# A deeper software pipeline and another weight conversion in a fused top-k attention and MLP kernel

## The chip, the cores and the metric

The kernel runs on one core of a Trainium2 chip. The metric is device time of one execution in microseconds (us). The kernel before took 1919.19 us (median of 3 runs, 1914.49 to 1919.27).

Engines are named as in the profile: PE is TensorE (matmuls and transposes; PEld its weight loads), DVE is VectorE, ACT is ScalarE, POOL is GpSimd, SP is SyncE, which here issues every DMA. Each engine works through its own instructions in a fixed order and waits in place when an operand or a buffer isn't ready, so what stands behind a waiting instruction waits too.

## The reference

Eight batches of eight heads, 576 positions, head size 64. Each row of scores keeps its 32 largest; the rest get weight zero. The attention output goes through an MLP with 512 inputs, 2048 hidden units and 512 outputs.

```python
scores = scale * np.matmul(q, k.transpose(0, 1, 3, 2))
kth = np.partition(scores, -top_k, axis=-1)[..., -top_k:-top_k + 1]
scores = np.where(scores >= kth, scores, -1000000000.0)
attn = np.exp(scores - np.max(scores, axis=-1, keepdims=True))
attn = attn / (np.sum(attn, axis=-1, keepdims=True) + 1e-09)
x = np.matmul(attn, v)            # then (B,H,S,D) -> (B*S, H*D)
h = x @ w_in
g = np.where(h >= 1, h, np.where(h <= -1, 0.0, (h + 1) ** 2 / 4))
return g @ w_out
```

The two weight matrices arrive as 64-bit floats. The kernel loads each number as two 32-bit words and builds a 32-bit float from them itself.

## The kernel before

**Steps.** A step is 128 query rows of a pair of heads (`hp`), or 64 tail rows of two pairs. There are 144 steps, 18 for each batch. `begin` (with `scores`, L221) makes the scores of a step on PE in two halves of 288 keys; ACT scales them out of PSUM into `s` (L224; a ring of three). `weights` is DVE's part: the maximum of each column pair (`more`, L238), four rounds of the eight largest values and their removal (L244, L251), the minimum of each pair (`less`, L256) and its eight largest (L259), the 32nd value (`kth`, L263), then the mask, which multiplies the exponentials by "score is at least kth" and sums them (L271), and the reciprocal of the sum (L276, L277). ACT computes the exponentials `e` (L248) as soon as the first maximum stands, and POOL divides `e` by its sum (L279). `transpose_w` turns `e` on PE (L290, L293; ACT copies to `wT` and `wTt`, L291, L294), and `values` multiplies with v (L305, L313; ACT copies to `xT`, L318, L320).

**MLP.** When all steps of a chunk (one or two tiles of 128 rows) are done, its MLP joins a list `pending` in units: 16 hidden groups `hidden(f)` (four matmuls over 128 or 256 columns, L336; ACT reads the result twice, L340 and L342; POOL finishes the activation, L343 to L345), then the output in pairs of f (`final`, L353, 512 columns).

**Order.** PE's and DVE's instructions are put out in program order; ACT, POOL and SP are ordered by a scheduler. The main loop runs over m, and in one turn puts out: the values of step m-2, the scores of step m+1, DVE's `weights` of step m, half of the MLP share, the weight transposes of step m-1, query and key transposes for later steps, the other half of the share. The share is the MLP work left over the turns left; `advance` puts out units while their cost is covered, and only those whose weight pieces are already converted.

**Weight conversion.** 64 pieces of 256 columns are converted while the first steps run; `weights` calls `between()` six times in a step and each call converts one piece. A piece has three operations on DVE (L85, L86, L90), two passes on POOL (L93, L94), two on ACT (L92, L97), and a last one on DVE (L99), which is put out after the next piece's first three. Four pieces are put out ahead of step 0.

**PSUM.** Eight banks: four for the tag "a", shared in rotation by scores, weight, key and query transposes and `po` (the values' result), three for `ph` (hidden), one for `py` (output).

**End.** After everything the largest entry of `excess` is found (L478 to L483), and a flag decides whether a slower variant runs; in these runs it doesn't.

## Time and profile before

| | |
|---|---|
| median of 3 runs | 1919.19 us (1914.49 to 1919.27) |
| the profiled execution | 1915.05 us, of which its span 1913.0 us |
| granted TensorE clock, mean | 0.942 |
| PE busy in the span | 1679.1 us (88%) |
| DVE busy | 1625.4 us (85%) |
| POOL busy | 1028.8 us (54%) |
| ACT busy | 977.1 us (51%) |
| DMA | 57.75 MB, mean 30 GB/s |
| chain that ended last | PE 53%, DVE 22%, POOL 13%, ACT 6% of the span |

The span runs from the first to the last instruction. Busy time is time in which an engine executed something; two engines can be busy at once. The granted clock is the share of full speed that the clock gate gave TensorE: at a lower one the same matmuls take longer and look busier. Matmuls are pipelined, so one busy engine can still hold several of them. A row such as `PE pw L290 <- POOL e L279` says that PE's instruction of line 290, writing `pw`, was released last by POOL's of line 279, writing `e`; the numbers behind it are total us, times and the longest. In a timeline a row has start, duration, engine, line, operation, what it writes and reads, and shapes.

### The profile page before, as it was taken

The numbers are of one execution on the slowest core, as the hardware profiler recorded it, in microseconds if no ns is written. First come the engines' busy times: TensorE is split into PE (matmuls) and PEld (weight loads), VectorE is DVE, ScalarE is ACT, GpSimd is POOL, SyncE is SP. The second block draws the span as 40 slices with busy tenths as digits, with TensorE's granted clock in tenths as the row PEclk, the third lists the DMA queues.
The fourth block names the chain that finished last, engine by engine and source line by source line (L and its number), as shares of the span: only waits on it lengthen the run. The fifth ranks groups of instructions, "written<-read, shape, count | busy, mean of one in ns | idle before, by whom it ended". The sixth has DMA issues, their size and how long they took to land.

```text
span 1913.0 us, 32251 instructions
## 1 busy us (share of the span) xinstructions
PE 1679.1 (88%) x10129; PEld 1160.1 (61%) x10129; DVE 1625.4 (85%) x5011; ACT 977.1 (51%) x2429; POOL 1028.8 (54%) x1772
## 2 busy tenths in 40 slices
PE   2346478898999999998999999998999999998998
PEld 1234255656676685767575776666676667666565
DVE  5998989999999799999898898989987879879640
ACT  4345455546455564655454655555455555445432
POOL 3567572725454672818283674637274554553553
PEclk8667679899999999999999999999999999998999
DMA  6222210011010000110010000110010000000000
GB/s 173 80 78 77 77 28 17 26 30 24 9 40 20 23 18 23 32 36 12 16 38 23 21 12 24 40 27 12 23 31 25 11 12 11 10 12 7 6 7 14
DMA packets 107445, 57.75 MB, mean 30 GB/s; under 512 B 86272, under 2 KB 94464, under 8 KB 107264
## 3 DMA queue, kind: packets, MB, share of 16 engines
q1 hardware_dynamic: 107264, 55.59, 10.6%
q8 instruction: 82, 1.34, 0.3%
q14 instruction: 99, 0.81, 0.1%
HBM read 46.14 MB, written 9.44 MB: 29 GB/s over the span
## 4 chain that ended last, share of the span: by engine, by line
PE 53%; DVE 22%; POOL 13%; ACT 6%; issue 5%; DMA 1%; POOLq 0%; SPq 0%; DVEq 0%; ACTq 0%
PE py L353 24%; PE ph L336 11%; PE sp L221 6%; DVE tops L244 6%; PE po L305 5%; DVE more L251 5%; PE pw L290 4%; POOL g L345 4%; POOL r L344 3%; POOL e L279 2%; POOL r L343 2%; DVE e L271 2%; DVE more L238 2%; DVE seconds L259 2%; DVE less L256 1%
## 5 line engine op out<-in xcount | busy, mean ns | idle before, releaser
L353 PE MATMUL py<-w_out,g 128*128 128x512 f32 x1152 | 534.7, 607 | 41.7 <-DVE w_out L99 37.1
L336 PE MATMUL ph<-xT,w_in 128*128 128x256 f32 (+1 forms) x2816 | 553.3, 353 | 3.9 <-ACT g L342 2.8
L336 PEld LDWEIGHTS ph<-xT,w_in 128*128 128x128 f32 x2816 | 466.4, 197 | 83.0 <-issue 29.4
L244 DVE MAX8 tops<-more 128x8 f32<-128x288 f32 x1152 | 468.5, 448 | 5.0
L353 PEld LDWEIGHTS py<-w_out,g 128*128 128x128 f32 x1152 | 209.2, 191 | 286.4 <-issue 219.8
L251 DVE MATCH_REPLACE8 more<-tops,more 128x288 f32<-128x288 f32 x864 | 375.9, 443 | 0.0
L279 POOL TENSOR_SCALAR e<-e,rz 128x576 f32<-128x576 f32 x288 | 242.4, 850 | 130.9 <-DVE rz L277 104.9
L340 ACT ACTIVATE r<-ph,half 128x256 f32<-128x256 f32 (+1 forms) x352 | 153.9, 437 | 264.2 <-POOL g L345 135.2
L264 POOL TENSOR_TENSOR excess<-seconds,kth 128x2 f32<-128x2 f32 x144 | 39.2, 273 | 417.3 <-DVE kth L263 416.4
L271 DVE SCALAR_TENSOR_TENSOR e<-s,kth,e 128x576 f32<-128x576 f32 x288 | 242.4, 875 | 23.1 <-ACT e L248 6.6
L345 POOL TENSOR_TENSOR g<-r,g 128x256 f32<-128x256 f32 (+1 forms) x352 | 246.7, 701 | 24.0
L291 ACT COPY wT<-pw 128x512 f32<-128x512 f32 x288 | 155.5, 594 | 202.3 <-PE pw L290 202.3
L290 PE MATMUL pw<-ident,e 128*128 128x128 f32 x1152 | 161.5, 284 | 110.6 <-POOL e L279 105.9
L248 ACT ACTIVATE e<-s,nmax 128x576 f32<-128x576 f32 x288 | 213.1, 786 | 75.2 <-POOL nmax L246 74.4
L238 DVE TENSOR_TENSOR more<-s 128x576 f32<-128x576 f32 x144 | 130.4, 905 | 139.0 <-ACT s L224 138.6
L344 POOL TENSOR_TENSOR r<-r 128x256 f32<-128x256 f32 (+1 forms) x352 | 230.4, 655 | 26.1
L290 PEld LDWEIGHTS pw<-ident,e 128*128 128x128 f32 x1152 | 138.0, 146 | 162.5 <-POOL e L279 118.2
L221 PE MATMUL sp<-kT,qT 64*128 64x288 f32 x1024 | 196.5, 442 | 34.7 <-ACT xT L318 26.4
L224 ACT ACTIVATE s<-sp 128x288 f32<-128x288 f32 x576 | 197.9, 417 | 40.7 <-PE sp L221 36.8
L343 POOL TENSOR_SCALAR r<-r 128x256 f32<-128x256 f32 (+1 forms) x352 | 155.4, 441 | 93.5 <-ACT r L340 93.2
L305 PEld LDWEIGHTS po<-wT,v_in 128*64 128x64 f32 x2048 | 118.0, 140 | 74.8 <-issue 40.0
L221 PEld LDWEIGHTS sp<-kT,qT 64*128 64x128 f32 x1024 | 109.1, 189 | 84.6 <-ACT xT L318 39.4
(61 smaller groups left out, 1592.7 us busy)
## 6 DMA issues: line engine op xcount, KB each, us to landing
q_in<-in_q_dram SPq DMA_DIRECT2D x32, 256.0 KB, 3.0
v_in<-in_v_dram SPq DMA_DIRECT2D x8, 1024.0 KB, 5.8
k_in<-in_k_dram SPq DMA_DIRECT2D x64, 128.0 KB, 3.0
raw<-in_moe_w_in_dram SPq DMA_DIRECT2D x32, 256.0 KB, 2.7
raw<-in_moe_w_out_dram SPq DMA_DIRECT2D x32, 256.0 KB, 2.8
out_dram<-y SPq DMA_DIRECT2D x32, 256.0 KB, 2.3
v_tail<-in_v_dram SPq DMA_DIRECT2D x16, 64.0 KB, 2.5
k_tl<-in_k_dram SPq DMA_DIRECT2D x8, 128.0 KB, 3.2
```

Source lines behind the costliest of these rows:

```text
L221: nc.tensor.matmul(o[:, a0 - c0:a1 - c0], qT[d, g, :], kT[d, g, k0:k0 + a1 - a0], start=True, stop=True)
L244: nc.vector.max(out=tops[:, i, r:r + 8], in_=src[:, i, :])
L248: nc.scalar.activation(e[:, i, :], s[:, i, :], AF.Exp, bias=nmax[:, i:i + 1])
L251: nc.vector.match_replace(out=rest[:, i, :], in_to_replace=tops[:, i, r:r + 8], in_values=src[:, i, :], imm_value=LOWEST)
L271: nc.vector.scalar_tensor_tensor(out=e[:, i, :], in0=s[:, i, :], scalar=last[:, i:i + 1], in1=e[:, i, :], op0=ALU.is_ge, op1=ALU.mult, acc ...
L279: nc.gpsimd.tensor_scalar(e[:, i, :], e[:, i, :], rz[:, i:i + 1], 1.0, ALU.mult, ALU.mult)
L290: nc.tensor.transpose(pt[:, c, :], w[:, i, main(i)][:, c * P:(c + 1) * P], ident)
L305: nc.tensor.matmul(po[j * D:(j + 1) * D], v_in[:, h, c, :] if c < NT else v_tl[0][:, h, :], wT[:, j, c, :] if c < NT else wTt, start=(c == ...
L336: nc.tensor.matmul(ph, w_in[:, kk, f * P:(f + 1) * P], xT[:, kk, 0:cw], start=(kk == 0), stop=(kk == NK - 1))
L344: nc.gpsimd.tensor_tensor(out=r, in0=r, in1=r, op=ALU.mult)
L345: nc.gpsimd.tensor_tensor(out=g[:, 0:cw], in0=r, in1=g[:, 0:cw], op=ALU.add)
L353: nc.tensor.matmul(py, gs[f][:, i * P:(i + 1) * P], w_out[:, f, :], start=(f == 0), stop=(f == NF - 1))
```

## The change

It has six parts.

1. **A further step between mask and transposes.** In turn m the weight transposes are those of step m-2 and the values those of step m-3 (before: m-1 and m-2). `e` gets three buffers. The MLP share of a turn is put out as a quarter, a quarter and a half, and query and key transposes now stand ahead of the weight transposes. `advance` has a second condition: it keeps running times of PE and DVE from constants, and puts out units also while PE's is short of the time at which the `e` to be transposed is done.
2. **The next step's pair maxima ahead of the mask.** `more` of step m+1 is put out before the mask of step m. `less` is written over `more`, which gets two buffers.
3. **An own bank for values.** `po` leaves the tag "a" for a bank of its own. `ph` becomes two tiles of one bank each, each holding two hidden groups, in place of three tiles of one group. `y` has one buffer instead of two.
4. **Another conversion.** A piece has one operation on DVE, one on ACT with a bias, one integer add on POOL and one more on ACT, then two on DVE. The last two of a piece are put out ahead of the next piece's first part. Seven pieces a step for four steps, then eight; two calls ahead of step 0 instead of four. `raw` has three buffers.
5. **Early first scores.** Keys of the first head pair are loaded first, the values of a batch after its last keys. The first step's scores are put out after the first of four key blocks, with ACT in program order for that part.
6. **The check of `excess`** is put out in the last turn but one, ahead of the last MLP units.

The core of the diff:

```diff
     def weight_piece(pool, dst, src):
-        raw = pool.tile([P, 2 * WC], U32, name="raw", bufs=2)
+        raw = pool.tile([P, 2 * WC], U32, name="raw", bufs=3)
...
-        nc.vector.tensor_scalar(top, hi, 3, 0x3FFFFFFF, ALU.logical_shift_left, ALU.bitwise_and)
-        nc.vector.scalar_tensor_tensor(out=top, in0=hi, scalar=0xC0000000, in1=top,
-                                       op0=ALU.bitwise_and, op1=ALU.bitwise_or)
-        nc.vector.tensor_scalar(unit, top, 0xFF800000, None, ALU.bitwise_and)
-        nc.scalar.activation(low, lo, AF.Copy, scale=2.0 ** -52)
-        nc.gpsimd.tensor_tensor(out=low, in0=low, in1=unit.bitcast(F32), op=ALU.mult)
-        nc.gpsimd.tensor_tensor(out=low, in0=low, in1=top.bitcast(F32), op=ALU.add)
+        nc.vector.tensor_scalar(bits, hi, 3, None, ALU.logical_shift_left)
+        nc.scalar.activation(units, lo, AF.Identity, bias=two, scale=2.0 ** -51)
+        nc.gpsimd.tensor_tensor(out=bits.bitcast(I32), in0=bits.bitcast(I32), in1=units.bitcast(I32), op=ALU.add)
         nc.scalar.activation(size, hi.bitcast(F32), AF.Abs)
         yield
-        nc.vector.scalar_tensor_tensor(out=dst, in0=size, scalar=1.125 * 2.0 ** -15, in1=low,
+        nc.vector.scalar_tensor_tensor(out=bits, in0=hi, scalar=0x80000000, in1=bits,
+                                       op0=ALU.bitwise_and, op1=ALU.bitwise_or)
+        nc.vector.scalar_tensor_tensor(out=dst, in0=size, scalar=1.125 * 2.0 ** -15, in1=bits.bitcast(F32),
                                        op0=ALU.is_ge, op1=ALU.mult)
...
             piece = weight_piece(pool, dst, src)
-            next(piece)
             if before is not None:
                 next(before, None)
-                yield
+            next(piece)
             before = piece
+            yield
...
         def keys_of(b):
-            v_in, v_tl = load_values(b)
...
+                if hp == NHP - 1:
+                    got["v"], got["v_tl"] = load_values(b)
...
+        def pairs(st):
+            s = st["s"]
+            st["more"] = more = att.tile([P, 2, SH], F32, name="more")
+            nc.vector.tensor_tensor(out=more, in0=s[:, :, 0:SH], in1=s[:, :, SH:S], op=ALU.max)
...
-            st["e"] = e = att.tile([P, 2, S], F32, name="e")
+            st["e"] = e = att.tile([P, 2, S], F32, name="e", bufs=3)
...
-                src = rest = more
+                src = rest = less = st["more"]
...
+            if paired and after is not None:
+                pairs(after)
             z = att.tile([P, 2], F32, name="z")
...
-            po = ps.tile([P, P], F32, name="po", tag="a", bufs=4)
+            po = ps.tile([P, P], F32, name="po", tag="po")
...
-                ph = ps.tile([P, CW], F32, name="ph", tag="ph", bufs=3)[:, 0:cw]
+                if f % 2 == 0:
+                    phs.append(ps.tile([P, 2, CW], F32, name="ph", tag="ph", bufs=2))
+                ph = phs[-1][:, f % 2, 0:cw]
...
-                    y = pool.tile([P, DM], F32, name="y", bufs=2)
+                    y = pool.tile([P, DM], F32, name="y", bufs=1)
...
+        K_TIME, PIECE_TIME, UNIT_TIME = 10.2, 1.3, 0.22
+        pe_time, dve_time, done = 8.0, 10.0, {}
+        def advance(amount, until=0.0):
             due += amount
-            while pending and pending[0][1] <= converted and due >= pending[0][0]:
+            while pending and pending[0][1] <= converted and (due >= pending[0][0] or
+                                                              pe_time + pending[0][0] * UNIT_TIME < until):
                 cost, _, work = pending.popleft()
-                due -= cost
+                due = max(due - cost, 0.0)
                 spent += cost
+                pe_time += cost * UNIT_TIME
                 work()
...
-        queries(0)
-        begin(0)
-        for _ in range(4):
-            convert()
+        with tc.manual_schedule(engines={mybir.EngineType.Activation}):
+            queries(0)
+            begin(0)
+            if paired:
+                convert()
+                convert()
+                pairs(state[0])
+            for _ in first:
+                pass
...
-        for m in range(n + 2):
-            if 2 <= m:
-                values(state[m - 2])
+        for m in range(n + 3):
+            if 3 <= m:
+                values(state[m - 3])
...
-                weights(state[m], convert)
-            advance(share / 2)
-            if 1 <= m <= n:
-                transpose_w(state[m - 1])
+                quota, before = (7 if m < 4 else 8), converted
+                def between():
+                    slots[0] += 1
+                    while converted - before < quota * slots[0] // 6 and converted < n_pieces:
+                        convert()
+                weights(state[m], state[m + 1] if m + 1 < n else None, between)
+                dve_time = max(dve_time, pe_time if m == 0 else 0.0) + K_TIME + PIECE_TIME * (converted - before)
+                done[m] = dve_time
+            advance(share / 4)
             queries(m + 2)
...
-            advance(share / 2)
+            advance(share / 4, done.get(m - 2, 0.0) + 2.5)
+            if 2 <= m <= n + 1:
+                pe_time = max(pe_time, done[m - 2] + 2.0) + 1.0
+                transpose_w(state[m - 2])
+            if m == n + 1 and paired:
+                judge(ps, att)
+            advance(share / 2, pe_time + 1.5)
```

## Prediction

> **What bounds the kernel now.** I read the page's 40 slices first, one digit for the busy tenths of a slice of 48 us.
>
> ```profile
> PE   2346478898999999998999999998999999998998
> DVE  5998989999999799999898898989987879879640
> PEclk8667679899999999999999999999999999998999
> ```
>
> In slices 2 to 6 VectorE (DVE) is at eight or nine tenths while TensorE (PE) is at two to six, on a granted clock of six to eight tenths; from slice 9 on PE is nearly always full. So there are two stages with two limits. The table of busy time by stage, cut at step boundaries, gives the sizes (columns: stage, length, then busy time and instructions of PE, weight loads, DVE, ACT, POOL, then granted clock).
>
> ```profile
> 0.00:30.56 30.56, 11.18 (x48) 8.09 (x48) 8.33 (x20) 14.50 (x34) 8.62 (x21) 1.00 0.77 202
> 30.56:140.76 110.20, 32.75 (x208) 24.70 (x208) 104.28 (x287) 45.63 (x119) 67.79 (x97) 0.62 0.32 88
> 140.76:252.00 111.24, 56.01 (x270) 34.85 (x270) 103.78 (x283) 48.18 (x125) 72.65 (x111) 0.70 0.24 71
> 252.00:327.00 75.00, 67.45 (x472) 48.86 (x472) 66.47 (x213) 42.26 (x110) 36.30 (x75) 0.93 0.06 17
> 327.00:1873.00 1546.00, 1480.65 (x8969) 1022.48 (x8970) 1341.63 (x4211) 815.63 (x2008) 825.58 (x1423) 0.98 0.08 21
> ```
>
> Before 30.56 no attention step has begun on DVE. From there to 252, ten steps plus the weight conversion fill DVE to 94%. After 327 PE is busy 1480.65 of 1546 us, so 65.3 us is all that better overlap can win there. The waits of PE after 324 us say what they are (total, times, longest).
>
> ```profile
> PE sp L221 <- ACT xT L318: 24.6, 21, 5.2
> PE pk L182 <- ACT wT L291: 11.8, 7, 3.8
> PE pw L290 <- POOL e L279: 9.1, 6, 3.1
> PE sp L221 <- ACT xT L320: 5.7, 6, 1.7
> PE py L353 <- ACT y L357: 4.6, 6, 0.9
> ```
>
> Last I read DVE's timeline for one converted weight piece, and for the pair maximum right after a piece and in a step without pieces.
>
> ```profile
> 100.85 0.28 DVE L85 TENSOR_SCALAR top<-raw 128x256 uint32<-128x256 uint32 x1
> 101.17 0.43 DVE L86 SCALAR_TENSOR_TENSOR top<-raw,top 128x256 uint32<-128x256 uint32 x1
> 101.63 0.29 DVE L90 TENSOR_SCALAR unit<-top 128x256 uint32<-128x256 uint32 x1
> 101.84 0.42 DVE L99 SCALAR_TENSOR_TENSOR w_in<-size,low 128x256 f32<-128x256 f32 x1
> 102.17 0.81 DVE L244 MAX8 tops<-more 128x8 f32<-128x288 f32 x2
> ...
> 116.54 1.29 DVE L238 TENSOR_TENSOR more<-s 128x576 f32<-128x576 f32 x1
> ```
> ```profile
> 302.06 0.76 DVE L238 TENSOR_TENSOR more<-s 128x576 f32<-128x576 f32 x1
> ```
>
> A piece takes 102.17 - 100.85 = 1.32 us, by starts 0.32 + 0.46 + 0.21 + 0.33. The same maximum takes 1.29 us beside POOL's second conversion pass (L94) and 0.76 without it.
>
> **The early stage, step by step.** Steps start on DVE (L238) at 30.56, 51.95, 73.34, 95.05, 116.54, 140.76, 166.02, 188.57, 210.06, 232.37, and step 16 at 322.75; a bare step takes 10.35 (302.06 to 312.41). A step with six pieces takes 21.5 = 10.35 + 6 x 1.32 + 3.2. The 3.2 are collisions with POOL, readable as 0.5 each on the pair maximum, the pair minimum and z, and about 1.4 on the last piece beside POOL's normalization of e.
>
> Start. The first key transpose (10.84) waits for a block issued only at 7.80, behind 1 MB of values. Now it is second in SP's queue: issue near 1.9, landing 2.95 later, transposes near 5. Copies as in the trace (two of 0.585, tail 0.74, queries 0.59), scores 3 us, so scores stand near 12 instead of 23. Then piece 0 goes through ACT (0.44), POOL (0.8) and DVE (0.46 + 0.33 + 0.32), so the first pair maximum starts near 14.5, 16 us earlier, but with one piece done instead of four. The values, moved behind the keys, are first used near 53; their 5.9 us are hidden, and lost if the first values wait for them. For later batches v_in (5.8 us) is issued some six steps later than now and still tens of us ahead of use.
>
> Pieces. DVE loses `unit`: 1.32 - 0.21 = 1.11 us. POOL loses one of two passes (788 and 836 ns). Its new integer add isn't in the trace: at least the one-input pass L343 on this shape (441 ns), at most both old passes (1624). I take 0.80, the nearest row being the old add. With 1624, POOL's load in an eight-piece step is 8 x 1.62 + 2.4 = 15.4 of 21 us, still hidden, but the collisions return, 1.4 x 9 = 13 us. ACT's conversion with a bias is priced as without (436; L340 has 437 with one; 422 to 594 by L97 and L291, off the path either way). The pair maximum now follows small operations, so its 0.5 goes. I take 2.3 of collisions instead of 3.2.
>
> Sum. Seven pieces: 10.35 + 7.8 + 2.3 = 20.4; eight: 21.5. 14.5 + 4 x 20.4 + 4 x 21.5 = 182; three pieces are left, 14.2, so 196. The first MLP tile cost steps 4 and 5 together 6.4 extra (24.2 and 25.3 against 21.5); I keep 6: 202. Seven bare steps more: step 16 starts at 275, not 322.75. PE's first two-tile hidden group starts at 329.77 now. After the change the scores ahead of it are those of step 19, whose buffer (three in the ring) is free only after the mask of step 16: 285.4 + 1.2, so 286.6, with two more steps' scores (2.4 us) already done. **Early gain: 43 + 2.4, say 46 us.** Cover: until then both single tiles must be done. Call a row what PE does up to one step's weight transposes. At full clock its scores, transposes and values take 3.8 us (1.2 + 1.2 + 1.4), a single tile 29 (16 hidden groups of 0.95, 16 output groups of 0.87: twelve L353 instructions in 5.3). Rows 8 to 15 of the changed PE order hold 29 + 8 x 3.8 + 3 for key and query transposes = 63 us between 197 and 286, which has room down to a clock of 0.7; below that each lost us is lost. The first tile is tight: in step 5 POOL has 16 x 1.16 (0.30 + 0.40 + 0.46) + 8 x 0.8 + 2.2 = 27 us, over the step's 21.5. If two steps stretch so, 11 us are lost on DVE, which waits for POOL's add.
>
> **The late stage.** The rows' MLP loads are almost those of before; only waits change. A bank of its own for `po` takes away the two waits of scores on xT (24.6 + 5.7), since a scores tile no longer reuses po's slot. Key transposes move ahead of the weight transposes, so they no longer reuse slots that wT still reads (11.8). The further step lets DVE be about two steps ahead, not one, at each transpose; light rows at a chunk boundary (3.8 us of PE against 10.4 of DVE) then eat a reserve and 9.1 goes. **That is 51 us.** New: in the 14 light rows the transposes follow the scores at once and wait for ACT's copies (L290 on L224: 3.7 us now in three waits, 1.7 the longest); between nothing and 14 x 1.7 = 24 us, I take 8, nearer to the 3.7. The pair maximum ahead of the mask waits earlier for scores: behind it stand mask, sums, POOL's e and PE's transposes. DVE waits 133 us there already, PE being late, and the transposes come two steps on, so I take nothing; the ends are -4 (less collision) and 9, the old e wait back. `ph` as two pairs leaves two to three groups in flight instead of three: nothing to twice the present 2.8. One `y` buffer waits for a 2.3 us store, tiles being 14 us or more apart: nothing; without that distance 36 x 2.3 = 83. The check of `excess` no longer stands after the last y (pt to flag, 0.8 us): 1 us.
>
> **Sum** against the profiled execution (1915.05: span 1913.0 and 2 around it): 1915 - 46 - 51 + 8 - 1 = **1825 us**. The median of the three runs, 1919.19, is 4 us above that execution.
>
> **Rivals.** (1) Both gains come, 1800 to 1850 by the bounds (13 + 11 up, the new waits and collisions down): 0.65. (2) More: no new waits, the other 14 us of late idle go too, collisions halve (1.2 x 8): 1793, chance 0.10. For it speaks that POOL has half the passes. (3) The late waits return in another place, ACT's queue being in order: +43, so 1825 + 43 = 1868, chance 0.10. For it: wT and s copies wait on PE 185 and 33 us, so ACT is itself only just behind. Against it: every removed wait has a buffer as its cause, not ACT's load (53%). (4) The early stage wins nothing, conversion being bound by POOL or loads: 1915 - 51 + 8 - 1 = 1871, chance 0.06. (5) **Slower:** the two halves of one `ph` bank serialize PE with ACT. Place: each odd hidden group. Price: ACT's two readings, 437 + 433 ns, 176 times: 153 us, so 1978; it decides from 90 / 176 = 0.51 us a pair. Against it: in the changed instruction order the odd group waits for nothing, and PE's group (1.79 us) is twice ACT's reading. Chance 0.06. (6) The reordering does nothing measurable: 0.03.
>
> The trace of before never has PE write a bank that ACT reads. The Trainium skill, PSUM — Partial Sum Buffer, section "PSUM bank collisions raise a hardware error", speaks against this part: two engines in one bank and the same partitions collide even at different columns, and the chip doesn't stall for it, so bank by bank waits are wanted. By the rule's "does not stall" the sum stays at 1825; with the waits it asks for, it would be rival 5's 1978. No run here shows it yet.
>
> **Numbers.** 1825 is the likeliest case. The range 1793 to 1868 holds cases 1 to 3 (0.85). About 0.3% (6 us) is what a measurement of this kernel can tell from no change. Faster 0.65 + 0.10 + 0.10 + 0.06 = 0.91, same 0.03, slower 0.06.
>
> **What would show it.** The first L238-like pair maximum near 14.5; pieces of 1.1 us; steps of 20 to 22 us until near 200; the first two-tile hidden group near 287; no wait of scores on xT; PE idle after it near 22 us instead of 65. I am wrong if steps with pieces take over 23 us, if PE waits on ACT's r or g in hidden groups, or if DVE, not PE, is full after 300.

## The result, and the profile after

The changed kernel takes **1963.36 us** (median of 4 runs, 1959.41 to 1964.24) against 1918.7 us before: ratio 1.0234, 95% interval [1.0213, 1.0254]. It is 2.3% slower; 1825 was predicted, and 1868 was the upper end. The profiled span is 1962.4 us at a mean clock of 0.952 (before: 1913.0 at 0.942).

The page's slices of the changed kernel, 49 us each:

```profile
PE   4365787989998999989998899979898998988987
DVE  5878899999997789897976788898976878669620
PEclk8566998999999999999999999999999999999999
```

The early stage did become shorter: TensorE's (PE's) first seven digits sum to 40 tenths instead of 34, on a similar clock. But of the 32 slices from the ninth on only 19 show a nine, before 27; in the others PE stands idle for a tenth of the time or more. The table of busy time by stage, cut at the changed kernel's step boundaries (columns: stage, length, busy time and instructions of PE, weight loads, DVE, ACT and POOL, granted clock, DMA share, GB/s):

```profile
0.00:14.57 14.57, 6.93 (x28) 4.67 (x28) 1.26 (x4) 7.50 (x16) 3.38 (x14) 1.00 0.86 220
14.57:114.40 99.83, 43.92 (x212) 31.05 (x212) 81.76 (x259) 55.29 (x134) 40.55 (x57) 0.61 0.45 126
114.40:206.11 91.71, 55.01 (x231) 36.53 (x231) 73.12 (x224) 46.65 (x117) 52.49 (x88) 0.68 0.27 84
206.11:287.73 81.62, 67.45 (x513) 48.81 (x514) 70.17 (x234) 46.61 (x120) 35.37 (x76) 0.98 0.09 22
298.00:1962.00 1664.00, 1504.01 (x9101) 1019.64 (x9099) 1312.40 (x4201) 829.92 (x2034) 814.57 (x1471) 0.99 0.07 19
```

The last row starts at PE's first hidden group of two tiles, at 298.40 us. In the kernel before that group starts at 329.77:

```profile
329.77 5.45 PE L336 MATMUL ph<-xT,w_in 128*128 128x256 f32 x24
```

This mark cuts every run here into two parts. What is called the late stage is the span less the mark: before 1913.0 - 329.8 = 1583 us, after 1962.4 - 298.4 = 1664 us. So the change **gains 31 us ahead of the mark and loses 81 us behind it**, where PE is idle for 1664 - 1504 = 160 us instead of 1583 - 1509 = 74. PE's waits at a hidden bank (`ph`) over the whole changed kernel (total, times, longest), and the same row of the kernel before, from 324 us on:

```profile
PE ph L344 <- ACT g L350: 156.6, 126, 4.1
```
```profile
PE ph L336 <- ACT g L342: 2.8, 4, 1.1
```

The row of 2.8 us in four waits has become 156.6 us in 126; 135.3 us in 111 waits lie behind the mark. The waits of scores on xT are gone, as predicted. The timeline of PE and ACT from the mark on shows one such wait (start, duration, then in brackets the idle time before it and what ended that):

```profile
298.40 1.99 PE L344 MATMUL ph<-xT,w_in 128*128 128x256 f32 x8
300.43 0.47 ACT L348 ACTIVATE r<-ph,half 128x256 f32<-128x256 f32 x1 [3.04 <-PE ph L344]
300.80 0.47 ACT L350 ACTIVATE g<-ph,minus 128x256 f32<-128x256 f32 x1
...
301.32 3.72 PE L344 MATMUL ph<-xT,w_in 128*128 128x256 f32 x16 [0.93 <-ACT g L350]
```

Eight matmuls fill the first half of a bank. Then PE stands until ACT has read that half twice (300.43 to 301.27) and starts the second half 0.05 us later. It is so in all 176 pairs: no second half starts less than 0.05 us after ACT's second reading has ended, and the first weight load of each carries a wait for the semaphore that ACT's L350 raises. All 126 waits stand ahead of a second half, none ahead of a first. That second half and the first half of the other bank follow each other without a break (x16), and then it begins again. The kernel before runs 24 matmuls, three groups, in one stretch (the row at 329.77 above).

### The profile page after: what moved, and what is told of

Its sections match the earlier page's. It is cut to its first block, busy times and chain, and to the rows that moved or that the text cites. A ratio compares the mean times of both kernels' runs of the same rounds, so it can differ in the third digit from the quotient of the medians.

```text
span 1962.4 us, 32038 instructions
## 1 busy us (share of the span) xinstructions
PE 1684.2 (86%) x10129; PEld 1145.8 (58%) x10129; DVE 1548.6 (79%) x4947; ACT 990.4 (50%) x2429; POOL 948.6 (48%) x1709
## 4 chain that ended last, share of the span: by engine, by line
PE 56%; DVE 17%; ACT 10%; POOL 10%; issue 5%; DMA 1%; DVEq 0%; SPq 0%; POOLq 0%; ACTq 0%
PE py L361 23%; PE ph L344 16%; PE sp L223 7%; PE po L311 6%; DVE tops L248 4%; DVE more L255 4%; PE pw L296 3%; DVE e L277 3%; ACT e L252 2%; ACT r L348 2%; POOL e L285 2%; POOL r L352 2%; POOL g L353 2%; ACT g L350 2%; POOL r L351 2%
## 5 line engine op out<-in xcount | busy, mean ns | idle before, releaser
L344 PE MATMUL ph<-xT,w_in 128*128 128x256 f32 (+1 forms) x2816 | 589.4, 361 | 156.9 <-ACT g L350 156.6
L285 POOL TENSOR_SCALAR e<-e,rz 128x576 f32<-128x576 f32 x288 | 215.7, 760 | 270.2 <-DVE rz L283 240.0
L234 DVE TENSOR_TENSOR more<-s 128x576 f32<-128x576 f32 x144 | 114.2, 793 | 236.2 <-ACT s L226 235.6
L353 POOL TENSOR_TENSOR g<-r,g 128x256 f32<-128x256 f32 (+1 forms) x352 | 241.0, 685 | 26.2 <-ACT g L350 0.9
L268 POOL TENSOR_TENSOR excess<-seconds,kth 128x2 f32<-128x2 f32 x144 | 53.6, 373 | 402.9 <-DVE kth L267 402.9
L351 POOL TENSOR_SCALAR r<-r 128x256 f32<-128x256 f32 (+1 forms) x352 | 160.3, 455 | 175.2 <-ACT r L348 174.7
L352 POOL TENSOR_TENSOR r<-r 128x256 f32<-128x256 f32 (+1 forms) x352 | 215.9, 613 | 25.4
L296 PE MATMUL pw<-ident,e 128*128 128x128 f32 x1152 | 155.8, 279 | 27.8 <-POOL e L285 22.8
L311 PE MATMUL po<-wT,v_in 128*64 128x128 f32 x2048 | 161.2, 290 | 15.8 <-ACT wT L297 14.3
L223 PE MATMUL sp<-kT,qT 64*128 64x288 f32 x1024 | 165.0, 442 | 1.0 <-ACT qT L205 1.0
```

Source lines behind the costliest of these rows:

```text
L223: nc.tensor.matmul(o[:, a0 - c0:a1 - c0], qT[d, g, :], kT[d, g, k0:k0 + a1 - a0], start=True, stop=True)
L285: nc.gpsimd.tensor_scalar(e[:, i, :], e[:, i, :], rz[:, i:i + 1], 1.0, ALU.mult, ALU.mult)
L296: nc.tensor.transpose(pt[:, c, :], w[:, i, main(i)][:, c * P:(c + 1) * P], ident)
L311: nc.tensor.matmul(po[j * D:(j + 1) * D], v_in[:, h, c, :] if c < NT else v_tl[0][:, h, :], wT[:, j, c, :] if c < NT else wTt, start=(c == ...
L344: nc.tensor.matmul(ph, w_in[:, kk, f * P:(f + 1) * P], xT[:, kk, 0:cw], start=(kk == 0), stop=(kk == NK - 1))
L352: nc.gpsimd.tensor_tensor(out=r, in0=r, in1=r, op=ALU.mult)
```

## The experiments

The theory: the two halves of one `ph` bank serialize PE with ScalarE (ACT), which is rival 5 of the prediction, with its place and mechanism. The rival: the removed waits come back elsewhere, behind ACT's in-order queue (rival 3), or the pair maxima ahead of the mask hold up the rest, and the pairing is only where the wait is seen. "The planner" in what follows is the scheduler that orders ACT, POOL and SP and puts waits between the engines. When the first group had settled that, later runs asked why the late stage did not gain even without the shared bank, and what each early part was worth.

All runs, in the order of their groups ("mark" is the first two-tile hidden group, "late" the span less the mark, both us of the one profiled run; each ratio is against the kernel before on the same chip):

| run | median us | ratio [95%] | mark | late |
|---|---|---|---|---|
| before | 1918.3 to 1919.7 | 1 | 329.8 | 1583 |
| changed | 1963.4 | 1.0234 [1.0213, 1.0254] | 298.4 | 1664 |
| a1: two single banks | 1884.0 | 0.9821 [0.9801, 0.984] | 299.4 | 1581 |
| a2: three, po with scores | 1903.5 | 0.9911 [0.9892, 0.9929] | 299.8 | 1603 |
| a3: three, po own | 1955.2 | 1.0186 [1.0169, 1.0203] | 306.8 | 1646 |
| b1: before + pairs in ph | 2001.7 | 1.0424 [1.0407, 1.0442] | 337.9 | 1663 |
| c1: a1, pair maxima in place | 1884.2 | 0.9822 [0.9806, 0.9839] | 302.6 | 1579 |
| c2: a1, no further step | 1917.9 | 0.9996 [0.9986, 1.0006] | 306.4 | 1609 |
| c3: a1, nmax on DVE | 1867.1 | 0.9733 [0.9717, 0.975] | 299.7 | 1566 |
| c4: c1 and c3 | 1895.3 | 0.9879 [0.9862, 0.9895] | 301.2 | 1592 |
| d1: a1, ACT in program order | 1902.9 | 0.9918 [0.9902, 0.9935] | 342.6 | 1559 |
| d2: a2, ACT in program order | 1915.3 | 0.9979 [0.997, 0.9989] | 340.8 | 1574 |
| d3: a1, old conversion | 1912.8 | 0.9974 [0.9962, 0.9985] | 326.7 | 1582 |
| d4: a1, start of before | 1892.5 | 0.9871 [0.985, 0.9892] | 306.4 | 1584 |
| e1: a1, ACT's order late only | 1904.0 | 0.9921 [0.9904, 0.9937] | 343.0 | 1557 |
| e2: a1, three r | 1886.7 | 0.9832 [0.9815, 0.9849] | 307.6 | 1577 |
| e5: e1, nmax on DVE | 1914.3 | 0.9974 [0.9961, 0.9986] | 345.4 | 1568 |
| e4: e5, three r | 1894.1 | 0.9864 [0.9848, 0.988] | 355.7 | 1539 |
| f2: a1, exponential after pieces | 1863.0 | 0.9707 [0.969, 0.9723] | 299.1 | 1565 |
| **f1: f2, nmax on DVE** | **1860.7** | **0.9695 [0.9679, 0.9711]** | 299.5 | 1561 |

### The bank of the hidden halves: a1 and b1

a1 is the changed kernel with each hidden group in a bank of its own, two of them; all else stays.

```diff
-                if f % 2 == 0:
-                    phs.append(ps.tile([P, 2, CW], F32, name="ph", tag="ph", bufs=2))
-                ph = phs[-1][:, f % 2, 0:cw]
+                ph = ps.tile([P, CW], F32, name="ph", tag="ph", bufs=2)[:, 0:cw]
```

> The changed kernel, with each hidden group alone in its PSUM bank: two tiles of one group in the same two banks, in place of two tiles of two groups. Theory A (the second group of a shared bank waits until ACT has read the first, though its columns are free): the wait of ph on ACT's g falls from 156.6 us to under 25, and the time to 1815-1850 us. Theory B (two banks are too few, or ACT is simply late by its order of work): as many banks, so the wait stays over 100 us and the time over 1920.

b1 is the opposite edit: the kernel before, with two tiles of two groups in place of three tiles of one. So it also has one bank less for `ph`.

> The kernel before with only the hidden tiles changed: two tiles of two groups, values still in tag a. Theory A: each second group waits about 1 us as in the changed kernel, so 100-160 us of ph waits and 2010-2080 us. Theory B, in the form that the shared banks hurt only together with the deeper pipeline's order on ACT: under 1960 us.

a1 takes 79 us off the changed kernel (1963.4 to 1884.0), though it has room for two groups instead of four; b1 adds some 82 us to the kernel before (2001.7). Both removal and addition move the time by about the same. That b1 has one bank less doesn't explain it: PE's waits at `ph` there, 128.1 us in 110, all stand ahead of a second half, none ahead of a first half, where a missing bank would show. So the shared bank **is** the cause of these 79 us. That the built program has the wait is shown; whether the planner puts it in because the halves are one tile or because they lie in one bank isn't, as no run has two separate tiles in a bank. In b1 the wait sits at the same place, behind the first eight matmuls of its mark (timeline of PE, first two rows):

```profile
337.86 1.99 PE L338 MATMUL ph<-xT,w_in 128*128 128x256 f32 x8
340.79 3.72 PE L338 MATMUL ph<-xT,w_in 128*128 128x256 f32 x16 [0.93 <-ACT g L344]
```

In a1 PE's wait at `ph` over the whole kernel is 71.4 us instead of 156.6: 85 us less wait, 79 us less time.

```profile
PE ph L342 <- ACT g L348: 71.4, 52, 3.6
```

So a1's wait isn't zero either, and its time lies between the ranges of both theories (A had under 25 us and 1815 to 1850). b1 is 8 us under its range. What holds a1 back is the second question.

### More hidden banks: a2 and a3

PSUM's eight banks are all in use. A third single bank for `ph` has to be taken from somewhere: a2 lets `po` share the four slots of scores and transposes again, as before the change; a3 leaves `po` its bank and cuts those four to three.

```diff
-            po = ps.tile([P, P], F32, name="po", tag="po")
+            po = ps.tile([P, P], F32, name="po", tag="a", bufs=4)     # a2
...
-                pt = ps.tile([P, NT, P], F32, name="pw", tag="a", bufs=4)
+                pt = ps.tile([P, NT, P], F32, name="pw", tag="a", bufs=3)     # a3, and all others of tag a
```

> The changed kernel with the PSUM part undone: hidden groups in three banks of their own, values back in the rotation of tag a. Theory A: ph's wait under 10 us, scores wait on xT about 30 us again, time 1830-1870. Theory B, in the form that ACT is late by its order: ph's wait stays over 60 us, time over 1900.

> The changed kernel with three banks of one hidden group each and a bank for values, tag a cut to three banks. Theory A: no ph wait (under 10), no wait of scores on xT, but scores and transposes may wait for ACT's copies in the shorter rotation: 1820-1870. Theory B: ph's wait stays over 60 us, over 1900.

Both are slower than expected, since each pays elsewhere. a2 has 26.8 us left at `ph`, but scores wait for xT again (30.0 + 14.4 us); late stage 1603. a3 has 26.1 us at `ph`, and scores wait 85.1 us for ACT's copies of s, 39.6 of them late; late stage 1646. The rest of a3's late loss isn't idle time: behind the mark its scores (L223) keep PE busy for 221.7 us, a1's for 139.5. Two single banks and an own bank for `po` is the best of the three divisions.

### Why the late stage gains nothing: c1 to c4

In a1 the late stage is 1581 us against 1583, though the three waits of the prediction (51 us) are gone. PE's waits in a1 from its mark on show what took their place:

```profile
PE ph L342 <- ACT g L348: 57.8, 44, 3.2
PE po L311 <- ACT wT L297: 10.1, 18, 2.1
PE py L359 <- ACT y L363: 5.3, 7, 0.9
```

One large wait of 57.8 us at `ph` stands where 24.6 + 5.7 on xT, 11.8 on wT and 9.1 on e were. Over the stage PE is idle for 91 us in a1, before for 74: the removed waits have come back with some more. The stage is no longer for it because PE is also busy for 20 us less (1489 instead of 1509). That lies in the scores, as rows of PE's instructions show (busy us, mean ns of one, idle time before them; before from 330 to 1830, a1 from 299 to 1830):

```profile
L221 PE MATMUL sp<-kT,qT 64*128 64x288 f32 x880 | 166.7, 438 | 28.5 <-ACT xT L318 23.2 <-ACT xT L320 5.1
```
```profile
L223 PE MATMUL sp<-kT,qT 64*128 64x288 f32 x884 | 139.7, 435 | 0.0
```

As many matmuls of the same mean length cover 27 us less, so before they lay further apart: eight of them take 1.24 us at 328.60 and 1.79 at 341.89. That fits waits inside a group of scores, which the profile counts as busy. a2, with `po` in the rotation again, has 168.0 us there from its mark on, a1 139.5. So a bank of its own for `po` seems to have removed more than the 30 us that show as waits on xT.

The cause of the wait at `ph` can be read on a1's timeline (DVE, POOL, ACT and PE; other rows are left out):

```profile
530.73 0.80 DVE L248 MAX8 tops<-more 128x8 f32<-128x288 f32 x2
...
532.01 1.47 POOL L285 TENSOR_SCALAR e<-e,rz 128x576 f32<-128x576 f32 x2
...
533.46 0.40 POOL L349 TENSOR_SCALAR r<-r 128x256 f32<-128x256 f32 x1
...
533.83 0.19 POOL L250 TENSOR_SCALAR nmax<-tops 128x2 f32<-128x2 f32 x1
...
534.05 1.44 ACT L252 ACTIVATE e<-s,nmax 128x576 f32<-128x576 f32 x2 [3.14 <-POOL nmax L250]
535.40 0.46 ACT L346 ACTIVATE r<-ph,half 128x256 f32<-128x256 f32 x1
535.76 0.46 ACT L348 ACTIVATE g<-ph,minus 128x256 f32<-128x256 f32 x1
...
536.27 1.99 PE L342 MATMUL ph<-xT,w_in 128*128 128x256 f32 x8 [1.01 <-ACT g L348]
```

ACT stands 3.14 us at an exponential that needs the negated row maximum (`nmax`). DVE has that maximum at 531.53, but POOL computes `nmax` only at 533.83, behind its normalization of e and work of the hidden layer. The hidden group was ready, but its two readings are behind the exponential in ACT's queue; the bank comes free at 536.22, and PE has stood 1.01 us.

Two theories for that lateness: P, the pair maxima ahead of the mask; Q, the row maximum in POOL's queue. c1 puts the pair maxima back at the head of their own step; c2 takes out the further step between mask and transposes; c3 moves nmax to VectorE (DVE); c4 is c1 and c3 together.

```diff
-                    nc.gpsimd.tensor_scalar(nmax, tops[:, :, 0], -1.0, 1.0, ALU.mult, ALU.mult)
+                    nc.vector.tensor_scalar(nmax, tops[:, :, 0], -1.0, 1.0, ALU.mult, ALU.mult)     # c3
...
-            if paired and after is not None:
-                pairs(after)     # c1: pairs(st) at the head of weights() instead
...
-        for m in range(n + 3):
-            if 3 <= m:
-                values(state[m - 3])
+        for m in range(n + 2):     # c2, and m - 2, m - 1 for m - 3, m - 2 below
+            if 2 <= m:
+                values(state[m - 2])
```

> The changed kernel with single hidden banks (as a1, 1884 us), and the pair maxima back at the head of their own step, behind the mask. Theory P (where PE is the limit, DVE waits at the pair maxima for scores, and the mask moved behind that wait, with POOL's normalization of e, stands between scores and exponentials, so that ACT waits in place at the exponentials and its readings of ph come late): ACT's wait of e on nmax after 330 us falls from 145 to under 80, ph's wait on g from 55 to under 20, time 1835-1860. Theory D (the further step alone has put ACT's work in an order that waits): both stay, 1875-1895.

> a1 without the further step: transposes of step m-1 and values of step m-2 again, the pair maxima ahead of the mask. Theory P: the wait of e on nmax stays over 120 us after 330 us, and PE waits for e more than in a1, so 1885-1930. Theory D: the wait of e on nmax falls under 90, ph's wait under 25, time 1840-1870.

> a1 with the negated maximum (128x2) on DVE in place of POOL, 144 operations of about 0.2 us on an engine that waits 150 us for scores. Theory Q (a part of P: the negated maximum stands in POOL's queue behind the normalization of e, 1.5 us, and activation passes): the wait before the exponentials, now on DVE, falls from 145 to 70-100 us after 330 us, ph's wait to 20-40, time 1850-1872. If POOL's queue has no part in it: 1880-1895.

> c1 and c3 together. Theories P and Q: no more than c1, or a few us better (1825-1855), for with the pair maxima in place the negated maximum is less often late. Theory D: as a1, 1875-1890.

P falls: c1 is as fast as a1 (1884.2 and 1884.0). But the waits that it names do shrink in c1, the exponential's from 145.1 to 108.8 us (330 to 1830) and PE's at `ph` from 57.8 to 44.8, and the time stays: less of this wait alone isn't yet a gain. Q holds in part: c3 gains 17 us, 15 of them late, with PE's wait at `ph` down to 44.1 us from the mark on; the exponential's wait falls to 114.9 us only, where 70 to 100 were expected. c4 is slower than either (1895.3); with nmax on DVE the place of the pair maxima does matter, and why was not followed up. c2 shows what the further step is worth: 34 us (7 ahead of the mark, 28 late). Without it the exponential's wait on nmax in the late stage is 248.5 us instead of 145.1, and `PE pw <- POOL e` is back with 8.4.

### ACT's order, and the early parts: d1 to d4

> a1 (single hidden banks, 1884 us) with ACT's instructions in program order throughout, where the scheduler ordered them. Theory O (the late stage gains nothing because ACT stands in place at the exponentials, which the scheduler put ahead of the readings of hidden groups, until DVE's first maxima are there): in program order the exponentials of a step come after the next step's scores but ahead of all MLP readings of that turn, when DVE is a step further, so ACT's wait of e on nmax after 330 us falls from 145 to under 50, ph's wait under 20, late stage (from the first two-tile hidden group to the end, 1581 us) under 1555, time 1835-1865. Theory R (two hidden banks are the reserve that is missing, whatever ACT's order): ph's wait stays at 45 or more, time 1875-1900. In the early stage program order may cost 0 to 15 us.

> a2 (three single hidden banks, values in tag a, 1903 us) with ACT in program order. Theory O: waits of ph and of scores on xT both fall, to under 15 and 30 us, time 1835-1870, near d1. Theory R: ph under 10 us, scores on xT 30 or more, 1870-1900.

The planner orders ACT's instructions; d1 gives them program order instead (the separate order of the start goes into it), d2 does so in a2.

```diff
-        order = tc.manual_schedule(engines={mybir.EngineType.PE, mybir.EngineType.DVE})
+        order = tc.manual_schedule(engines={mybir.EngineType.PE, mybir.EngineType.DVE, mybir.EngineType.Activation})
```

The late stage falls by 22 us in d1 (1559) and by 30 in d2 (1574), but the mark moves from 299 to 343 us, so both lose. Ahead of the mark POOL's add waits 47.6 us for ACT's `units` (a1: 29.8), and DVE 67.1 us for POOL's add, 26.1 the longest (a1: 32.1). These two don't say whether the late gain is ACT's order or only the larger lead that other engines have when PE is late.

> a1 with the weight conversion of before (four operations on DVE, two passes on POOL, the last operation behind the next piece's first three), with the new numbers of pieces per step. By the prediction's terms a piece costs DVE 0.21 us more (13 us in all) and collisions come back (0.9 x 9 = 8 us), so 1900-1910. If the new conversion's own waits (DVE for POOL's add 30 us, for loads 12 us) ate its gain: 1878-1892.

> a1 with the start of before: values loaded ahead of keys, all four key blocks ahead of the first scores. By the prediction the first pair maximum comes some 12-16 us later, and as no piece is converted meanwhile all of it is lost: 1894-1902. If the load of weights or POOL sets the early stage: under 1890.

d3 is a1 with the conversion of before, d4 with keys and values loaded as before; d3 ends 3 us above its expected range, d4 between its two. The mark moves by 27.3 us in d3 and by 7.0 in d4, the time by 28.8 and 8.5. Of a1's 30 us gain ahead of the mark the conversion is the main part. (With 7 from the further step in c2 the three add up to 41; they overlap.)

### What holds the bank: e1 to f2

> The hidden halves in two single banks, and ScalarE's instructions put in program order from step 11 on; before that the planner orders them as in a1. Theory O (in the late stage ScalarE stands at an exponential, waiting for its row maximum, while pieces of the hidden layer queue behind it; program order lets them pass): first two-tile hidden group near 300 us as in a1 (299.38), late stage near 1559 us as in d1 (1558.6) instead of 1581, time 1855 to 1872 us. Rival (program order gains late only because of what it lost early, the queues being further apart): late stage 1575 us or more, time 1880 us or more.

> The hidden halves in two single banks, three buffers for r instead of two (raw has two instead of three to make room, which may cost a few us before step 16; so the late stage alone is judged). Theory S (the relu on ScalarE stands because r's two buffers are still being read by GpSimd, 116.6 us of waits in a1, and the hidden bank is let go late for that): late stage under 1570 us against 1581, ScalarE's wait at r on GpSimd's g under 40 us, PE's wait at ph under 50 us against 71.4. Rival O (ScalarE's order is what holds the bank): late stage 1577 to 1585 us, PE's wait at ph as in a1, ScalarE's time at r only moved to another wait.

> e1 with the negated maximum on VectorE in place of GpSimd. If the two gains stand apart (a1's late stage of 1581 us became 1566 with nmax on VectorE alone, 1559 with ScalarE's order alone): late stage near 1545 us, time 1840 to 1858 us. If both take away the same wait (exponential on nmax, 26.0 us left in d1 of 145): late stage 1555 to 1560 us, time as e1 within 6 us.

> e5 with three buffers for r and two for raw. Under S, with ScalarE in program order and 198 us of waits at r on GpSimd in d1, the third buffer takes another 10 us or more: late stage 1535 us or less. Under O alone it is worth nothing late and loses a few us early to raw: late stage as e5 within 5 us, time 0 to 10 us above e5.

```diff
+        late = tc.manual_schedule(engines={mybir.EngineType.Activation})     # e1, e5, e4
...
+            if m == 11:     # ACT in program order from here
+                late.__enter__()
...
-                r = pool.tile([P, CW], F32, name="r", bufs=2)[:, 0:cw]
+                r = pool.tile([P, CW], F32, name="r", bufs=3)[:, 0:cw]     # e2, e4; raw has 2 instead of 3
```

e1 didn't test what it was for: ACT's instructions stand in d1's order from the first to the last, its mark is at 343.0, and it repeats d1 (1904.0 and 1902.9). e2 says that r's buffers aren't the cause in the planner's order: ACT's wait at r on POOL falls from 108.2 to 23.2 us (300 to 1862), its wait at the exponential rises from 151.1 to 179.8, and PE's wait at `ph` from the mark on stays at 55.3 us (a1: 57.8), the late stage at 1577; S falls there. With ACT in program order they are: e4's late stage is 30 us shorter than e5's, and ACT's wait at r on POOL falls from 220.8 to 78.8 us (20 us in the whole time, as the mark moves 10 us back). Every kernel of this order pays 41 us or more ahead of the mark. nmax on DVE gains nothing in it: e5 is 10 us slower than e1 (late 1568 and 1557), which neither expectation had, and why is open.

f2 leaves ACT's order to the planner, with one rule more, late only: an exponential stands behind the last hidden piece that was issued before it. f1 is f2 with nmax on DVE.

```diff
-                        nc.scalar.activation(e[:, i, :], s[:, i, :], AF.Exp, bias=nmax[:, i:i + 1])
+                        ex = nc.scalar.activation(e[:, i, :], s[:, i, :], AF.Exp, bias=nmax[:, i:i + 1])
+                        if m >= 14 and last_g:
+                            tc.add_manual_dep(ex.ins, last_g[-1].ins.name, mybir.DependencyInfo(
+                                mybir.DependencyClass.NoSync, mybir.DependencyReason.DATA), reason="order")
...
-                nc.scalar.activation(g[:, 0:cw], ph, AF.Relu, bias=minus, scale=1.0)
+                last_g[:] = [nc.scalar.activation(g[:, 0:cw], ph, AF.Relu, bias=minus, scale=1.0)]
```

> a1 with one rule more for the planner: from step 14 on, an exponential stands behind the last hidden piece issued before it in ScalarE's order; ScalarE's order up to there is a1's (the first 490 rows of the built order agree). Theory O (the exponential that waits for its row maximum holds the hidden pieces behind it, and so the bank): first two-tile hidden group at 299 to 301 us as in a1, PE's wait at ph on g in the late stage under 40 us against 57.8 to 71.4, the exponential's wait on nmax under 60 us against 145, late stage 1560 to 1570 us, time 1864 to 1874 us. Rival (the hidden pieces are late for r's buffers and ScalarE's own load, the exponential only stands in time that is free): late stage 1577 us or more, time 1880 us or more, the wait at r on GpSimd up by what the exponential's falls.

> f2 with the negated maximum on VectorE (c3, 1867.1 us, with the same rule more). If VectorE's maximum gained because ScalarE stands shorter at the exponential, the two take away the same wait: time within 6 us of the better of f2 and c3 (1864 to 1874 us). If they add up (15 us for nmax, 10 to 20 for the order): 1850 to 1860 us. Under the rival to O: as c3, or slower by up to 10 us.

f2 has its mark where a1 has it (299.1) and a late stage of 1565 us instead of 1581: 1863.0 us, 21 us under a1. So the planner's place for the exponential does hold the hidden bank (Theory O). PE's wait and two of ACT's waits in f2 from 300 us on:

```profile
PE ph L347 <- ACT g L353: 41.2, 38, 3.0
```
```profile
ACT r L351 <- POOL g L356: 163.4, 128, 4.2
...
ACT e L254 <- POOL nmax L252: 105.7, 53, 4.6
```

The same rows of ACT in a1, from 300 us on:

```profile
ACT e L252 <- POOL nmax L250: 151.1, 66, 4.9
...
ACT r L346 <- POOL g L351: 108.2, 97, 3.5
```

The sizes expected weren't reached: the wait at `ph` is 41.2 us, not under 40, and the exponential's is 105.7, not under 60. ACT's wait at r on POOL rises by 55 as the exponential's falls by 45; this is what the rival said of ACT. But PE's wait at `ph` falls by 17, and the time with it. f1's 1860.7 us is the fastest time here (ratio 0.9695 [0.9679, 0.9711]), but its interval overlaps f2's: nmax on DVE, worth 17 us without the rule, adds 2.3 to it. The two take away mostly the same wait. In f1 PE is idle for 75 us late, as before the change (74): its late gain of 22 us is in PE's busy time (1486 instead of 1509 us), mostly in that of the scores, as in a1 (138.8 us).

## Why the prediction was wrong

**The step that failed** is the dismissal of rival 5: "in the changed instruction order the odd group waits for nothing". It does wait. Every second half of a bank has a wait on ACT ahead of its first matmul, put into the program by the planner; the trace shows PE held by it 126 times, 1.24 us each. The term "`ph` as two pairs: nothing to twice the present 2.8" measured 79 us in the changed kernel (some 82 in the kernel before, with one bank less). Rival 5 had place and mechanism right, and the prediction's own sign of being wrong, "if PE waits on ACT's r or g in hidden groups", is what came. Rival 5's price, 153 us of waits, is nearly the 156.6 measured, but only 79 of them are time: a1 waits 71.4 us at `ph` without the sharing. Rival 5's other objection, "PE's group (1.79 us) is twice ACT's reading", is true and irrelevant: a wait between two groups costs ACT's reading however long the group is. A chance of 0.06 was too small for it. The prediction had put two sums beside the rule of the Trainium skill, PSUM — Partial Sum Buffer, section "PSUM bank collisions raise a hardware error": 1825 without waits, 1978 with the waits that it asks for. The program has these waits, in all 176 pairs. That 1963 came out near 1978 is in part luck, though: the waits cost 79 us instead of 153, and the rest of the miss has other causes. What would happen without the waits wasn't tried.

**The late gain of 51 us** failed too, in a1 as in the changed kernel. Each wait named did go. For two of the three the cause given was tested and right: with `po` in the rotation (a2) the waits on xT are back, without the further step (c2) the wait on e; the key transposes' 11.8 us weren't tested alone. But the sum took "gone" for "won". As much came back, most of it at `ph`, as rival 3 had it: 1581 us in a1 against 1583 - 51 + 8 = 1540. That "every removed wait has a buffer as its cause, not ACT's load" was no argument against it, since ACT needn't be loaded to be late: it stood at an exponential. With the order mended (f2) 18 of the 43 us come. "65.3 us is all that better overlap can win" was no bound either: PE's busy time, which the sum took as fixed, falls late by 20 us in a1.

**The early gain** was 31 us, not 46. Point by point: the first pair maximum is at 14.57 (14.5 predicted). A piece costs 1.08 us (1.11 predicted), read from DVE's timeline by starts, 94.73 - 93.65:

```profile
93.65 0.42 DVE L96 SCALAR_TENSOR_TENSOR bits<-raw,bits 128x256 uint32<-128x256 uint32 x1
94.18 0.43 DVE L98 SCALAR_TENSOR_TENSOR w_in<-size,bits 128x256 f32<-128x256 f32 x1
94.53 0.28 DVE L87 TENSOR_SCALAR bits<-raw 128x256 uint32<-128x256 uint32 x1
94.73 0.16 DVE L282 TENSOR_SCALAR z<-z 128x2 f32<-128x2 f32 x1
95.71 0.42 DVE L96 SCALAR_TENSOR_TENSOR bits<-raw,bits 128x256 uint32<-128x256 uint32 x1 [0.62 <-POOL bits L91]
```

The last row shows a wait that the sum had at nothing: the next piece stands 0.62 us for POOL's add. The add itself is as cheap as assumed (0.72 us at 94.96, 0.80 taken), and the pair maximum takes 0.74 instead of 1.29 us. (The 1.29 us row lay beside both of POOL's passes, 0.67 us of L93 and 0.53 of L94, not L94 alone; and the clock of slices 2 to 6 was six to seven tenths, with PE at three to seven.) But DVE now runs closer behind. Its waits in the changed kernel up to 288 us:

```profile
DVE bits L96 <- POOL bits L91: 29.9, 31, 5.1
DVE bits L87 <- DMA raw<-in_moe_w_in_dram: 11.5, 2, 8.1
DVE more L234 <- ACT s L226: 9.3, 1, 9.3
```

and those of the kernel before up to 323 us:

```profile
DVE top L85 <- DMA raw<-in_moe_w_in_dram: 20.0, 3, 18.3
DVE w_out L99 <- POOL low L94: 6.9, 4, 2.7
DVE more L238 <- ACT s L224: 5.3, 2, 2.9
```

A good part of these stands ahead of the first pair maximum, where the earlier start already counts it. From there on DVE waits 37.9 us in the changed kernel, 24.8 of them for POOL's add and 9.3 for scores, and 13.6 in the kernel before. The prediction had "11 us are lost on DVE, which waits for POOL's add" as an upper case and took nothing. Yet the steps with pieces lose little by it: step 9 starts at 206.11 (202 predicted), so other terms of these steps were smaller than assumed. The larger loss is one bare step, which waits 9.3 us for scores at 246.62: PE puts them out at 244.48, behind hidden groups that waited 8.0 us for ACT from 222.62 to 241.26, where the prediction had said that its cover "has room". In a1, with single banks, this step waits as long (9.6). So step 16 starts at 287.73 instead of 275. Alone, the start of loading is worth 7 us (d4); the prediction gave it 16 less three pieces, about 13.

**Terms that held**: pair maxima ahead of the mask at nothing (c1: 0.2 us of 1884), the waits of scores on xT gone. Of the new waits of weight transposes on scores 8 us were taken; they measure 3.3 us late (pw 2.3 and its tail 1.0, in a1 and in the changed kernel), no more than the 4.8 before.

**The sum**: 1825 + 79 (bank) + 41 (late stage of a1, 1581 instead of 1540) + 15 (early) = 1960, against 1963.4. The 41 and the 15 are themselves differences of measured and predicted, so that the sum closes proves nothing; the 79 us are shown by a1 and b1, and f2 shows the cause of some 16 of the 41. What stays open: the rest of the 41, what exactly spreads the scores in the kernel before, and how the 36.6 us that f1 still waits at `ph` divide between r's buffers and the exponential.

## What to carry to other kernels

Two halves of one tile in one PSUM bank worked as one buffer here: count the wait of the second on the readers of the first as ACT's reading times the pairs (153 us against 156.6 measured; only half of it was time), and look for that wait at the first instruction of the second half. A wait that a buffer removes is a gain only if the engine that frees the next buffer isn't late too; before counting it, read that engine's queue for an instruction that stands in it for a third engine (here ACT's exponential, for POOL's row maximum), since it holds all that is queued behind it. Then compare times, not waits: in c1 this wait shrank and the time stayed. A rule for the order of two instructions in that queue was worth 21 us of 1884, the same wait taken at its source (nmax on DVE) 17, both together 23.

## What the runs showed of the hardware

The hand-over within a shared bank takes next to nothing by itself: 0.05 us lie between the end of ACT's second reading (301.27) and PE's next matmul (301.32). The price is ACT's two readings and what stands before them in its queue. In the changed kernel and in b1 no matmul of a second half starts before ACT's readings of the first have ended (176 of 176 pairs in each), so no trace here shows PE writing one half of `ph` while ACT reads the other.

POOL's addition of integers on 128 x 256 takes 0.72 to 0.73 us with DVE idle or at its maximum search, and 1.10 to 1.11 beside DVE's pair maximum or pair minimum; DVE's own row isn't longer for it (0.75). In the kernel before, the same pair maximum took 1.28 to 1.29 us beside POOL's two float passes.

PE's granted clock in the DVE-bound stage is 0.61 and 0.68 (before 0.62 and 0.70) and 0.98 in the next row, where MLP work helps to keep PE busy for 67.45 of 81.62 us. At the reduced clock PE is busy 44 to 60% of the stage and DVE 80 to 82%.
